# FFT filter and gated FFN in one kernel: the second transform stage as three products of rounded parts, and PSUM banks dealt out three and three

## The chip, the cores and the metric

The kernel runs on one core of one Trainium2 chip. The metric is the time of one execution on the device, in microseconds. Engines are named as in the profile: PE (TensorE, matmuls; PEld are its weight loads), DVE (VectorE), ACT (ScalarE), POOL (GpSimd), and SP (SyncE, which here issues nearly all DMAs).

## The reference

The input `x` has 8 batches of 3136 tokens by 256 channels. Along the tokens a real FFT is taken, multiplied by a complex filter per channel, and transformed back; then comes a gated feed-forward block:

```python
X = np.fft.rfft(x, axis=1)
y = np.fft.irfft(X * (filt_r + 1j * filt_i)[None], n=3136, axis=1)
h = np.maximum(y @ w_in, 0.0)                       # 256 -> 1024
conv_out[:, i] = sum(conv_w[k] * h[:, i + k - 1] for k in range(3))   # along tokens, zeros outside
out = (h / (1 + np.exp(-conv_out))) @ w_out          # 1024 -> 256
```

## The kernel before, in words

**Transforms.** 3136 is 112 x 28, and each batch goes through four stages of matmuls. Stage 1 multiplies by a 112x112 table for each of 28 columns, stage 2 by a small matrix `s2_sb` (112x120, its variant `s2s_sb` for the last column), then the filter is applied, stage 3 multiplies by `s3_sb`/`s3s_sb`, and stage 4 turns the result into `y`, channels on partitions. Each stage is cut into 14 operations of two columns (`NP = 14`). Stage 1 and stage 3 write their results to DRAM (`a_dram`, `b_dram`), since stages 2 and 4 read them in another order. All four stages are plain f32 matmuls; in the trace each f32 matmul stands as two rows.

**Products of parts.** The feed-forward block works on numbers split in two: a high part rounded to f32r by ACT (`hi_act`, L156) and the rest by DVE or POOL (`lo_dve` L159, `lo_pool` L162), both f32r. `mm3` (L186 to L189) multiplies by three matmuls: high by high, high by low, low by high.

**The main loop** (L680) runs over steps m. The tokens of all batches are cut into units of 510 (`UO`); a unit takes 8 steps, one for each 128 of the 1024 inner channels, and a window of 48 steps belongs to one batch. In each step:

- `inner` (L484): 6 matmuls of 512 columns into a bank of the PSUM pool `ps_h`, 4 banks, on PE (L187 to L189, out `ps_h`);
- `relu` and `centre` (ACT, L495 and L500; centre writes the tile `t`, 4 buffers), two taps (DVE, L504), `sigmoid` (ACT, L507), `gate` (DVE, L510, the last reader of the `ps_h` bank, two steps after the inner product), `round_g` (ACT, L156) and `rest_g` (POOL, L162, the last reader of `t`);
- six steps later `project` (L529): 12 matmuls of 256 columns (L536 to L538); after each eighth step `evacuate` copies the output on DVE (L549) and stores it.

Each engine runs its instructions in the order in which the loop issues them (`manual_schedule`), SP's DMAs too.

**The transforms of the next batch** are spread over the steps by a planner (L570 to L600). Window t (t = 1 to 7) holds stages 2 to 4 of batch t and stage 1 of batch t+1, the last window's 48 and more steps hold none. In the second to seventh window stage 2 stands in steps 2, 3, 5, 7, 9, 11, 12, 14, 16, 18, 20, 21, 23 and 25, each stage 3 operation three steps after its stage 2, stage 4 in steps 33 to 44, and stage 1 of the next batch (not in the seventh window) in steps 0, 1, 4, 6, 8, 10, 13, 22, 27, 29, 30, 31, 32 and 45. In the first window two operations of stage 1 of batch 1 stand in each of steps 0 to 5, and stage 2 is denser, two of every three steps from 9 on, often beside a stage 3. Within a step the order is:

```python
for op in old:          # transforms of the step before
    from_bank(op)       # 1, 3: ACT copy (L240) and store; 2: filter on DVE (L264-L266) and POOL (L267); 4: DVE copy (L663)
want_in()               # loads of inputs
for op in new:
    transform(op)       # matmuls into a bank of ps_t
inner(...)
```

`transform` (L631) takes a bank of the PSUM pool `ps_t`, 2 banks, and `from_bank` (L652) empties it one step later. `want_in` (L613) keeps up to five inputs loaded ahead in the tile `tin` (5 buffers); tables and filters are loaded a few operations ahead (`want_table`, `want_filter`). The matmul lines of the transforms are L245 (stage 1), L249 and L252 (stages 2 and 3) and L275 (stage 4), all with out `ps_t`.

**Before the main loop** a prologue transforms batch 0, does two operations of stage 1 of batch 1, and converts the weights. The last quarter of the weights is converted in the first steps of the main loop (`late`).

Of the kernel before, what the change touches and what calls it, by code (L numbers as in the profile page):

```python
# [9 lines left out]
F32 = mybir.dt.float32  # L10
F32R = mybir.dt.float32r
# [121 lines left out]
def tile_fft_filter_gated_ffn(  # L133
# [21 lines left out]
    def hi_act(dst, src):  # L155
        nc.scalar.activation(dst, src, AF.Copy)  # L156
# [33 lines left out]

    dram = ctx.enter_context(tc.tile_pool(name="dram", bufs=1, space=bass.MemoryType.DRAM))
    a_dram = [dram.tile([N2, 112, D], F32, name=f"a_dram{b}") for b in range(B)]
    b_dram = [dram.tile([N2, 112, D], F32, name=f"b_dram{b}") for b in range(B)]
    a_out = [t[:].rearrange("n p d -> p n d") for t in a_dram]
    a_in = [t[:].rearrange("n (r g) d -> (n r) g d", g=G) for t in a_dram]
    b_out = [t[:].rearrange("n (r g) d -> (n r) g d", g=G) for t in b_dram]
    b_in = [t[:].rearrange("n p d -> p n d") for t in b_dram]
    xt = x.rearrange("b (p n) d -> (b p) n d", n=N2)
# [2 lines left out]
    wc = ctx.enter_context(tc.tile_pool(name="wc", bufs=1))  # L201
    s2_sb = wc.tile([112, 120], F32, name="s2_sb")
    s2s_sb = wc.tile([112, 120], F32, name="s2s_sb")
    s3_sb = wc.tile([120, 112], F32, name="s3_sb")
    s3s_sb = wc.tile([120, 112], F32, name="s3s_sb")
    one_sb = wc.tile([128, 128], F32, name="one_sb")
    cw = wc.tile([128, 3, NF], F32, name="cw")
    nc.gpsimd.memset(cw[:, 0, 0:1], 0.0)
    nc.scalar.activation(cw[:, 0, 0:1], cw[:, 0, 0:1], AF.Sigmoid)
# [20 lines left out]
    def pair(q):  # L230
        return slice(2 * q, 2 * q + 2)

    def load_in(pool, kind, b, q, bufs, tag):
        r = pool.tile([112, 2, D], F32, name=tag, bufs=bufs)
        nc.sync.dma_start(out=r, in_={"1": xv, "2": a_in, "4": b_in}[kind][b][:, pair(q)])
        return r

    def store(pool, kind, b, q, ps, bufs, tag, queue=nc.sync):
        st = pool.tile([112, 2, D], F32, name=tag, bufs=bufs)
        nc.scalar.activation(st, ps[0:112].rearrange("p (j d) -> p j d", d=D), AF.Copy)  # L240
        queue.dma_start(out={"1": a_out, "3": b_out}[kind][b][:, pair(q)], in_=st)

    def by_column(ps, w, r):
        for j in range(2):
# [8 lines left out]

    def second(ps, q, r):
        by_row(ps[0:120], q, r, s2_sb, s2s_sb)

    def third(ps, q, z):
        by_row(ps[0:112], q, z, s3_sb, s3s_sb)
# [24 lines left out]
    conv_raw = tp.tile([128, 1, 6 * NF], I32, name="conv_raw", bufs=1)  # L283

    def load_weights(k, pool):
        raws[k] = raw = pool.tile([128, 2, 1024], I32, name="raw", bufs=1 if pool is tp else 2)
        for part, w in enumerate((w_in, w_out)):
            nc.sync.dma_start(out=raw[:, part], in_=w[:, 1024 * k:1024 * k + 1024])

# [3 lines left out]
        e, m = (em[:, i, 0:1, 0:n] for i in range(2))  # L293
        yield from to_f32(cw.rearrange("p (o k) f -> p o (k f)", o=1), conv_raw, e, m)

    def convert(k, pool, n=2):

        for j in range(2):
            em = pool.tile([128, 2, 2, 256], I32, name="em", bufs=n)
            w = pool.tile([128, 2, 256], F32, name="ws", bufs=n)  # L300
            yield from to_f32(w, raws[k][:, :, 512 * j:512 * j + 512], em[:, 0], em[:, 1])
            halves = [(t[0][:, j, 256 * k:256 * k + 256], t[1][:, 2 * k + j]) for t in zip(wi, wo)]
            for part in range(2):
                nc.gpsimd.tensor_copy(halves[0][part], w[:, part])
            for part in range(2):
                lo_pool(halves[1][part], w[:, part], halves[0][part])
# [5 lines left out]
    with (  # L312
# [2 lines left out]
        tc.manual_schedule(engines=COMPUTE | {mybir.EngineType.SP}),  # L315
    ):
        fts, tabs, rows, zs, pss = {}, {}, {}, {}, {}
        by_r = [sc.tile([120, 4, N2], F32, name=f"by_r{i}", bufs=1) for i in range(2)]
        bt = sc.tile([128, KT, G, 112], F32, name="bt", bufs=1)

# [30 lines left out]
        with tc.tile_pool(name="sq", bufs=2) as sq:  # L351
# [14 lines left out]

            def first_loads(c):
                table("1", c)
                r = sq.tile([128, 4, D], F32, name="rows", bufs=5)
                nc.sync.dma_start(out=r, in_=xt[0:128, 4 * c:4 * c + 4])  # L370
                rows["x", c] = r[0:112]
                if c in (0, 3):
                    load_weights(c // 3, sc)
                if c == 1:
                    nc.sync.dma_start(out=conv_raw[:, 0], in_=conv_w)
                if c == 4:
                    for dst, t in ((one_sb, one), (s2_sb, s2[:, 0:120]), (s2s_sb, s2s[:, 0:120]), (s3_sb, s3), (s3s_sb, s3s)):
                        nc.sync.dma_start(out=dst, in_=t)
# [16 lines left out]
            for i in range(NP + 4):  # L395
                if i < NP:
                    back = [at[:, k].rearrange("p n (r g) -> p (n r) g", g=G) for k in range(KT)]
                    rows["2", i] = turn_back(lambda j, k: back[k][:, :, 2 * i + j], sq, "ar")
                if 0 <= i - 1 < NP:
                    pss[i - 1] = ps = bank()  # L400
                    second(ps, i - 1, rows.pop(("2", i - 1)))
                if 0 <= i - NP < AHEAD:
                    ps = bank()
                    by_column(ps, tab("1", i - NP), rows.pop(("1", i - NP)))
                    store(tp, "1", 1, i - NP, ps, 3, "st", nc.scalar)
                if 0 <= i - 4 < NP:
                    q = i - 4
                    ps = turned_stage(zs.pop(q), [by_r[q == NP - 1 and j].rearrange("p r c -> p (r c)") for j in range(2)])
                    nc.scalar.activation(bt[:, :, pair(q)], ps, AF.Copy)
                if 0 <= i - 2 < NP:  # L410
                    zs[i - 2] = filt(pss.pop(i - 2), i - 2, fts.pop(i - 2))
                    if i + 2 < NP:
                        load_filter(i + 2)
                if i == 5:
                    table("1", 0)
                    for q in range(AHEAD):
                        r = sq.tile([128, 2, D], F32, name="xa", bufs=2)
# [24 lines left out]

    yps.append(ctx.enter_context(tc.tile_pool(name="y_odd", bufs=1, reuse_waits="tile")))
    wp = ctx.enter_context(tc.tile_pool(name="wp", bufs=2, reuse_waits="tile"))
    ps_h = ctx.enter_context(tc.tile_pool(name="ps_h", bufs=4, space=bass.MemoryType.PSUM, reuse_waits="tile"))
    ps_t = ctx.enter_context(tc.tile_pool(name="ps_t", bufs=2, space=bass.MemoryType.PSUM, reuse_waits="tile"))
    ps_o = ctx.enter_context(tc.tile_pool(name="ps_o", bufs=1, space=bass.MemoryType.PSUM, reuse_waits="tile"))

    outf = out.rearrange("b s d -> (b s) d")
    LEN = B * ROW - 1  # L450
    NU = -(-LEN // UO)
    ts, hs, gs, pos, joined = {}, {}, {}, {}, {}
    ring = [[wp.tile([128, UO + 66], F32R, name=f"g{i}{h}", bufs=1) for h in range(2)] for i in range(4)]
    for pair_of in ring:
        for g in pair_of:
            nc.gpsimd.memset(g[:, UO:UO + 2].bitcast(F32), 0.0)
# [154 lines left out]
        return kind == "1" or stored.get(({"2": "1", "4": "3"}[kind], b), 0) == NP  # L611

    def want_in():  # L613
        while wanted["in"] < min(done["in"] + 5, len(inputs)) and ready(inputs[wanted["in"]]):
            op = inputs[wanted["in"]]
            wanted["in"] += 1
            got_in[op] = load_in(tp, *op, 5, "tin")

    def want_table(n):
        for op in tables[n:n + 1]:  # L620
# [10 lines left out]
    def transform(op):  # L631
        kind, b, q = op
        banks[op] = ps = ps_t.tile([128, 512], F32, name="ps_t")
        if kind in "124":
            done["in"] += 1
            r = got_in.pop(op)
        if kind in "14":
            want_table(done["table"] + 3)
            done["table"] += 1
            w = got_table.pop(op)  # L640
        if kind == "1":
            by_column(ps, w, r)
        if kind == "2":
            want_filter(done["filter"] + 1)
            done["filter"] += 1
            second(ps, q, r)
        if kind == "3":
            third(ps, q, got_z.pop((b, q)))
        if kind == "4":
            fourth(ps, r, w)  # L650

    def from_bank(op):  # L652

        kind, b, q = op
        ps = banks.pop(op)
        if kind in "13":
            store(tp, kind, b, q, ps, 3, "st")
# [16 lines left out]
    with tc.manual_schedule(engines=COMPUTE | {mybir.EngineType.SP}):  # L674
# [1 line left out]
        for n in range(3):  # L676
            want_table(n)
        want_filter(0)
        late = convert(3, wp, 1)
        for m in range(NF * NU + PLAG + 1):  # L680
            p1, p2, p3, p4, p6, p7 = (at(m - k) for k in (1, 2, 3, 4, PLAG, PLAG + 1))
            new, old = plan.get(m, []), plan.get(m - 1, [])
            if p7:
                evacuate(*p7)
            for op in old:
                from_bank(op)
            want_in()
# [72 lines left out]
```

## Time and profile before

| | |
|---|---|
| median of 3 runs | 1554.89 us (1553.32 to 1556.66) |
| the profiled execution's own time | 1554.59 us |
| its span in the trace | 1552.8 us |
| mean granted TensorE clock | 0.997 |
| first inner product | at 88.85 us |
| bytes moved by DMA | 229.49 MB, mean 148 GB/s |
| HBM read and written | 157.10 MB and 70.65 MB |

The span is what the trace covers; the 1.8 us between it and the execution's own time lie around it. Times in rows are microseconds from the start of the span, a row's second number is its duration, and "x2" means that neighbouring rows were merged. Square brackets give the idle time of the engine before a row and what ended it. Rows of groups give busy time in us and the mean of one in ns, then idle time before them. The ends of matmuls are modelled, so matmul rows overlap; the distance of their starts tells the pace.

### The profile page before, as it was taken

What the parts mean: (1) busy time and instruction counts of PE and PEld (TensorE: products, weight loads), DVE (VectorE), ACT (ScalarE), POOL (GpSimd) and SP (SyncE); (2) the same over time, 40 slices, a digit from 0 to 9 for tenths busy, and PEclk for the clock granted to TensorE, in tenths of its full rate; (3) what the DMA queues carried; (4) which work ended last, traced back from release to release, by engine and by line L of the source; (5) the groups of instructions that cost most, each with busy time, mean ns of one, the idle gap of its engine ahead of it and who ended that gap; (6) DMA issues with size and microseconds to landing.
All of it is one profiled execution on the core that took longest, in us unless ns stands there. A gap on an engine that the chain in (4) does not pass through costs nothing.

```text
span 1552.8 us, 26446 instructions
## 1 busy us (share of the span) xinstructions
PE 1519.7 (98%) x9202; PEld 1290.6 (83%) x9202; DVE 1185.3 (76%) x1810; ACT 1144.7 (74%) x1973; POOL 828.3 (53%) x721
## 2 busy tenths in 40 slices
PE   6999999999999999999999999999999999999999
PEld 5777788877997789877898778987799878999998
DVE  7978766788677877778777776778867888777776
ACT  3576668766896668866787667976688667888886
POOL 4644447545574555645565445744557445664444
PEclk9999999999999999999999999999999999999999
DMA  8867653665436555465544665356543543300000
GB/s 302 256 185 215 208 170 109 181 200 166 135 110 202 179 155 159 121 193 169 177 124 143 185 196 153 97 179 203 165 135 100 160 140 110 101 28 15 28 28 30
DMA packets 158436, 229.49 MB, mean 148 GB/s; under 512 B 16432, under 2 KB 109088, under 8 KB 158304
## 3 DMA queue, kind: packets, MB, share of 16 engines
q1 hardware_dynamic: 157824, 227.35, 48.4%
q8 instruction: 73, 1.20, 0.3%
q14 instruction: 59, 0.48, 0.1%
q10 hardware_dynamic: 480, 0.46, 0.1%
HBM read 157.10 MB, written 70.65 MB: 147 GB/s over the span
## 4 chain that ended last, share of the span: by engine, by line
PE 92%; DVE 2%; ACT 2%; DMA 2%; issue 2%; SPq 0%; POOL 0%; ACTq 0%; POOLq 0%; DVEq 0%
PE ps_h L187 12%; PE ps_h L189 12%; PE ps_h L188 12%; PE po L536 12%; PE po L538 12%; PE po L537 11%; PE ps_t L249 10%; PE ps_t L275 6%; PE ps_t L245 5%; DMA rows<-in_x 1%; PE ps_t L252 1%; ACT br L346 0%; DVE v L265 0%; DVE z L264 0%; DMA f<-in_filt 0%
## 5 line engine op out<-in xcount | busy, mean ns | idle before, releaser
L504 DVE SCALAR_TENSOR_TENSOR t<-ps_h,cw,t 128x510 f32<-128x510 f32 (+1 forms) x800 | 589.1, 737 | 301.5 <-ACT t L500 298.4
L162 POOL TENSOR_TENSOR g<-t,g 128x510 fp32r<-128x510 f32 (+1 forms) x400 | 505.3, 1273 | 203.6 <-ACT g L156 191.9
L536 PE MATMUL po<-wo,g 128*128 128x256 f32 (+1 forms) x1576 | 440.4, 279 | 0.1
L538 PE MATMUL po<-wo,g 128*128 128x256 f32 (+1 forms) x1576 | 439.5, 279 | 0.0
L537 PE MATMUL po<-wo,g 128*128 128x256 f32 (+1 forms) x1576 | 439.3, 279 | 0.0
L495 ACT ACTIVATE ps_h<-ps_h 128x512 f32<-128x512 f32 (+1 forms) x400 | 234.7, 587 | 243.9 <-PE ps_h L189 242.2
L500 ACT ACTIVATE t<-ps_h,cw 128x510 f32<-128x510 f32 (+1 forms) x400 | 272.4, 681 | 102.8 <-POOL g L162 70.1
L267 POOL TENSOR_TENSOR z<-z,v 120x512 f32<-120x512 f32 x112 | 144.8, 1293 | 380.4 <-DVE v L266 312.7
L187 PE MATMUL ps_h<-y,wi 128*128 128x512 f32 (+1 forms) x688 | 333.4, 485 | 0.5 <-DVE y L159 0.5
L536 PEld LDWEIGHTS po<-wo,g 128*128 128x128 f32 (+1 forms) x1576 | 297.0, 188 | 17.3 <-ACT g L156 0.3
L537 PEld LDWEIGHTS po<-wo,g 128*128 128x128 f32 (+1 forms) x1576 | 296.4, 188 | 17.0
L538 PEld LDWEIGHTS po<-wo,g 128*128 128x128 f32 (+1 forms) x1576 | 296.6, 188 | 0.6 <-POOL g L162 0.5
L189 PE MATMUL ps_h<-y,wi 128*128 128x512 f32 (+1 forms) x688 | 270.1, 393 | 0.0
L188 PE MATMUL ps_h<-y,wi 128*128 128x512 f32 (+1 forms) x688 | 270.1, 393 | 0.0
L510 DVE TENSOR_TENSOR t<-ps_h,t 128x510 f32<-128x510 f32 (+1 forms) x400 | 268.6, 671 | 0.9 <-ACT t L507 0.8
L507 ACT ACTIVATE t<-t 128x510 f32<-128x510 f32 (+1 forms) x400 | 245.3, 613 | 1.7 <-DVE t L504 1.6
L156 ACT ACTIVATE g<-t 128x510 fp32r<-128x510 f32 (+1 forms) x400 | 245.1, 613 | 0.2 <-DVE t L510 0.2
L162 POOL TENSOR_TENSOR y<-z,y 128x448 fp32r<-128x448 f32 x98 | 138.5, 1422 | 93.8 <-ACT y L156 91.9
L187 PEld LDWEIGHTS ps_h<-y,wi 128*128 128x128 f32 x688 | 130.4, 189 | 44.3 <-issue 23.6
L188 PEld LDWEIGHTS ps_h<-y,wi 128*128 128x128 f32 x688 | 130.7, 190 | 41.3 <-issue 24.3
L189 PEld LDWEIGHTS ps_h<-y,wi 128*128 128x128 f32 x688 | 130.0, 189 | 30.2 <-POOL wi L162 0.3
L240 ACT ACTIVATE st<-ps_t 112x512 f32<-112x512 f32 x194 | 114.0, 590 | 11.2 <-PE ps_t L245 11.1
(91 smaller groups left out, 1608.0 us busy)
## 6 DMA issues: line engine op xcount, KB each, us to landing
filt<-in_filt SPq DMA_DIRECT2D x98, 512.0 KB
tin<-a_dram SPq DMA_DIRECT2D x98, 224.0 KB
b_dram<-st SPq DMA_DIRECT2D x98, 224.0 KB
tin<-b_dram SPq DMA_DIRECT2D x98, 224.0 KB
tin<-in_x SPq DMA_DIRECT2D x96, 224.0 KB
a_dram<-st SPq DMA_DIRECT2D x96, 224.0 KB
out<-ot SPq DMA_DIRECT2D x45, 256.0 KB
tab<-in_m SPq DMA_DIRECT2D x98, 98.0 KB
```

Source lines behind the costliest of these rows:

```text
L156: nc.scalar.activation(dst, src, AF.Copy)
L162: nc.gpsimd.tensor_tensor(out=dst, in0=src, in1=hi.bitcast(F32), op=ALU.subtract)
L187: nc.tensor.matmul(ps, lhsT=wh, rhs=rh, start=start, stop=False, **kw)
L188: nc.tensor.matmul(ps, lhsT=wh, rhs=rl, start=False, stop=False, **kw)
L189: nc.tensor.matmul(ps, lhsT=wl, rhs=rh, start=False, stop=stop, **kw)
L500: nc.scalar.activation(t, hs[u, f][:, 1:n + 1], AF.Copy, scale=cw[:, 1, f:f + 1])
L504: nc.vector.scalar_tensor_tensor(out=t, in0=h[:, k:place(u)[2] + k], scalar=cw[:, k, f:f + 1], in1=t, op0=ALU.mult, op1=ALU.add)
L507: nc.scalar.activation(ts[u, f], ts[u, f], AF.Sigmoid)
L510: nc.vector.tensor_mul(ts[u, f], hs.pop((u, f))[:, 1:place(u)[2] + 1], ts[u, f])
L536: nc.tensor.matmul(o, lhsT=gh[:, c:c + n], rhs=wo[0][:, f], start=first, stop=False, skip_group_check=True)
L537: nc.tensor.matmul(o, lhsT=gh[:, c:c + n], rhs=wo[1][:, f], start=False, stop=False, skip_group_check=True)
L538: nc.tensor.matmul(o, lhsT=gl[:, c:c + n], rhs=wo[0][:, f], start=False, stop=last, skip_group_check=True)
```

## The change

From the third batch on (b = 2 to 7, six batches of 14 operations) the second stage is done with `mm3`: three f32r matmuls of parts in place of one f32 matmul. The parts of its input are made where the first stage's sums leave PSUM: ACT's copy becomes `hi_act` into the first half of a new tile `sh` (2 buffers), DVE makes the rest with `lo_dve` from the PSUM bank into the second half, and both halves are stored and loaded, by way of a second DRAM tensor `r_dram`. The matrices are split on POOL at step 8. Batches 0 and 1 keep the f32 form.

The PSUM pools change from 4 and 2 banks (`ps_h`, `ps_t`) to 3 and 3.

To make room in SBUF, buffers are dealt out anew: inputs of stage 2 have the tile `tia` (3 buffers), those of stages 1 and 4 `tin` (3 buffers, was 5 for all), stage 3's copies `st` (2 buffers, was 3 for stages 1 and 3); the late weight conversion borrows `tia` and `st`; the prologue's `rows` has 4 buffers (was 5). `want_in` looks six ahead in place of five but holds at most three inputs of either kind, and stops at the first that has no room.

```diff
-    def load_in(pool, kind, b, q, bufs, tag):
-        r = pool.tile([112, 2, D], F32, name=tag, bufs=bufs)
-        nc.sync.dma_start(out=r, in_={"1": xv, "2": a_in, "4": b_in}[kind][b][:, pair(q)])
+    def load_in(pool, kind, b, q):
+        if kind == "2" and b == 1:
+            r = pool.tile([112, 2, 2, D], F32R, name="tia", bufs=3)[:, 0].bitcast(F32)
+            nc.sync.dma_start(out=r, in_=a_in[b][:, pair(q)])
+            return r
+        if kind == "2":
+            r = pool.tile([112, 2, 2, D], F32R, name="tia", bufs=3)
+            for h, t in enumerate((a_in, r_in)):
+                nc.sync.dma_start(out=r[:, h].bitcast(F32), in_=t[b][:, pair(q)])
+            return r
+        r = pool.tile([128, 2, D], F32, name="tin", bufs=3)[0:112]
+        nc.sync.dma_start(out=r, in_={"1": xv, "4": b_in}[kind][b][:, pair(q)])
         return r
...
+    def store_first(pool, b, q, ps, queue=nc.sync):
+
+        st = pool.tile([112, 2, 2, D], F32R, name="sh", bufs=2)
+        p = ps[0:112].rearrange("p (j d) -> p j d", d=D)
+        hi_act(st[:, 0] if b > 1 else st[:, 0].bitcast(F32), p)
+        queue.dma_start(out=a_out[b][:, pair(q)], in_=st[:, 0].bitcast(F32))
+        if b > 1:
+            lo_dve(st[:, 1], p, st[:, 0])
+            queue.dma_start(out=r_out[b][:, pair(q)], in_=st[:, 1].bitcast(F32))
+
+    def store_third(pool, b, q, ps):
+        st = pool.tile([128, 2, D], F32, name="st", bufs=2)[0:112]
         nc.scalar.activation(st, ps[0:112].rearrange("p (j d) -> p j d", d=D), AF.Copy)
-        queue.dma_start(out={"1": a_out, "3": b_out}[kind][b][:, pair(q)], in_=st)
+        nc.sync.dma_start(out=b_out[b][:, pair(q)], in_=st)
...
+    def second_split(ps, q, r):
+
+        if q < NP - 1:
+            mm3(ps[0:120], *second_parts[0], *(r[:, h].rearrange("p j d -> p (j d)") for h in range(2)))
+        else:
+            for j, parts in enumerate(second_parts):
+                mm3(ps[0:120, j * D:j * D + D], *parts, r[:, 0, j], r[:, 1, j])
...
-                r = sq.tile([128, 4, D], F32, name="rows", bufs=5)
+                r = sq.tile([128, 4, D], F32, name="rows", bufs=4)
...
-    ps_h = ctx.enter_context(tc.tile_pool(name="ps_h", bufs=4, space=bass.MemoryType.PSUM, reuse_waits="tile"))
-    ps_t = ctx.enter_context(tc.tile_pool(name="ps_t", bufs=2, space=bass.MemoryType.PSUM, reuse_waits="tile"))
+    ps_h = ctx.enter_context(tc.tile_pool(name="ps_h", bufs=3, space=bass.MemoryType.PSUM, reuse_waits="tile"))
+    ps_t = ctx.enter_context(tc.tile_pool(name="ps_t", bufs=3, space=bass.MemoryType.PSUM, reuse_waits="tile"))
...
-        while wanted["in"] < min(done["in"] + 5, len(inputs)) and ready(inputs[wanted["in"]]):
+        while wanted["in"] < min(done["in"] + 6, len(inputs)) and ready(inputs[wanted["in"]]):
             op = inputs[wanted["in"]]
+            if sum((o[0] == "2") == (op[0] == "2") for o in got_in) == 3:
+                break
             wanted["in"] += 1
-            got_in[op] = load_in(tp, *op, 5, "tin")
+            got_in[op] = load_in(tp, *op)
...
-            second(ps, q, r)
+            (second_split if b > 1 else second)(ps, q, r)
...
+            if m == NF:
+                for (h, l), t in zip(second_parts, (s2_sb, s2s_sb)):
+                    nc.gpsimd.tensor_copy(h, t)
+                    lo_pool(l, t, h)
```

More of the change, by code (lines that the diff above doesn't have):

```diff
@@ L192, in tile_fft_filter_gated_ffn @@
     a_dram = [dram.tile([N2, 112, D], F32, name=f"a_dram{b}") for b in range(B)]
+    r_dram = [dram.tile([N2, 112, D], F32, name=f"r_dram{b}") for b in range(B)]
     b_dram = [dram.tile([N2, 112, D], F32, name=f"b_dram{b}") for b in range(B)]
-    a_out = [t[:].rearrange("n p d -> p n d") for t in a_dram]
-    a_in = [t[:].rearrange("n (r g) d -> (n r) g d", g=G) for t in a_dram]
+    a_out, r_out = ([t[:].rearrange("n p d -> p n d") for t in ts] for ts in (a_dram, r_dram))
+    a_in, r_in = ([t[:].rearrange("n (r g) d -> (n r) g d", g=G) for t in ts] for ts in (a_dram, r_dram))
     b_out = [t[:].rearrange("n (r g) d -> (n r) g d", g=G) for t in b_dram]
@@ L203, in tile_fft_filter_gated_ffn @@
     s2s_sb = wc.tile([112, 120], F32, name="s2s_sb")
+    second_parts = [[wc.tile([112, 120], F32R, name=f"{n}{h}") for h in range(2)] for n in ("s2", "s2s")]
     s3_sb = wc.tile([120, 112], F32, name="s3_sb")
     s3s_sb = wc.tile([120, 112], F32, name="s3s_sb")
-    one_sb = wc.tile([128, 128], F32, name="one_sb")
     cw = wc.tile([128, 3, NF], F32, name="cw")
@@ L231, in pair @@
         return slice(2 * q, 2 * q + 2)
-    def load_in(pool, kind, b, q, bufs, tag):
-        r = pool.tile([112, 2, D], F32, name=tag, bufs=bufs)
-        nc.sync.dma_start(out=r, in_={"1": xv, "2": a_in, "4": b_in}[kind][b][:, pair(q)])
-        return r
-    def store(pool, kind, b, q, ps, bufs, tag, queue=nc.sync):
-        st = pool.tile([112, 2, D], F32, name=tag, bufs=bufs)
+    def load_in(pool, kind, b, q):
[10 more added lines that the diff above has]
+        nc.sync.dma_start(out=r, in_={"1": xv, "4": b_in}[kind][b][:, pair(q)])
+        return r
+    def store_first(pool, b, q, ps, queue=nc.sync):
[8 more added lines that the diff above has]
+        st = pool.tile([128, 2, D], F32, name="st", bufs=2)[0:112]
         nc.scalar.activation(st, ps[0:112].rearrange("p (j d) -> p j d", d=D), AF.Copy)
-        queue.dma_start(out={"1": a_out, "3": b_out}[kind][b][:, pair(q)], in_=st)
+        nc.sync.dma_start(out=b_out[b][:, pair(q)], in_=st)
     def by_column(ps, w, r):
@@ L285, in load_weights @@
     def load_weights(k, pool):
-        raws[k] = raw = pool.tile([128, 2, 1024], I32, name="raw", bufs=1 if pool is tp else 2)
+        if pool is tp:
+            raws[k] = [pool.tile([128, 2, 2, D], F32R, name="tia", bufs=3).rearrange("p a j d -> p a (j d)").bitcast(I32) for _ in range(2)]
+            for j in range(2):
+                for part, w in enumerate((w_in, w_out)):
+                    nc.sync.dma_start(out=raws[k][j][:, part], in_=w[:, 1024 * k + 512 * j:1024 * k + 512 * j + 512])
+            return
+        raws[k] = raw = pool.tile([128, 2, 1024], I32, name="raw", bufs=2)
         for part, w in enumerate((w_in, w_out)):
@@ L294, in convert_conv, with convert @@
         yield from to_f32(cw.rearrange("p (o k) f -> p o (k f)", o=1), conv_raw, e, m)
-    def convert(k, pool, n=2):
+    def convert(k, pool):
         for j in range(2):
-            em = pool.tile([128, 2, 2, 256], I32, name="em", bufs=n)
-            w = pool.tile([128, 2, 256], F32, name="ws", bufs=n)
-            yield from to_f32(w, raws[k][:, :, 512 * j:512 * j + 512], em[:, 0], em[:, 1])
+            if pool is tp:
+                if j == 0:
+                    em = pool.tile([128, 2, 2, D], F32R, name="tia", bufs=3).bitcast(I32)
+                w, raw = pool.tile([128, 2, D], F32, name="st", bufs=2), raws[k][j]
+            else:
+                em = pool.tile([128, 2, 2, 256], I32, name="em", bufs=2)
+                w, raw = pool.tile([128, 2, 256], F32, name="ws", bufs=2), raws[k][:, :, 512 * j:512 * j + 512]
+            yield from to_f32(w, raw, em[:, 0], em[:, 1])
             halves = [(t[0][:, j, 256 * k:256 * k + 256], t[1][:, 2 * k + j]) for t in zip(wi, wo)]
@@ L317, in tile_fft_filter_gated_ffn @@
         fts, tabs, rows, zs, pss = {}, {}, {}, {}, {}
+        one_sb = sc.tile([128, 128], F32, name="one_sb", bufs=1)
         by_r = [sc.tile([120, 4, N2], F32, name=f"by_r{i}", bufs=1) for i in range(2)]
@@ L404, in tile_fft_filter_gated_ffn @@
                     by_column(ps, tab("1", i - NP), rows.pop(("1", i - NP)))
-                    store(tp, "1", 1, i - NP, ps, 3, "st", nc.scalar)
+                    store_first(tp, 1, i - NP, ps, nc.scalar)
                 if 0 <= i - 4 < NP:
@@ L416, in tile_fft_filter_gated_ffn @@
                     for q in range(AHEAD):
-                        r = sq.tile([128, 2, D], F32, name="xa", bufs=2)
+                        r = tp.tile([128, 2, D], F32, name="tin", bufs=3)
                         nc.sync.dma_start(out=r, in_=xt[N1:N1 + 128, pair(q)])
@@ L452, in tile_fft_filter_gated_ffn @@
     ts, hs, gs, pos, joined = {}, {}, {}, {}, {}
-    ring = [[wp.tile([128, UO + 66], F32R, name=f"g{i}{h}", bufs=1) for h in range(2)] for i in range(4)]
+    ring = [[wp.tile([128, UO + 2], F32R, name=f"g{i}{h}", bufs=1) for h in range(2)] for i in range(4)]
     for pair_of in ring:
@@ L655, in from_bank @@
         ps = banks.pop(op)
+        if kind == "1":
+            store_first(tp, b, q, ps)
+        if kind == "3":
+            store_third(tp, b, q, ps)
         if kind in "13":
-            store(tp, kind, b, q, ps, 3, "st")
             stored[kind, b] = stored.get((kind, b), 0) + 1
@@ L678, in tile_fft_filter_gated_ffn @@
         want_filter(0)
-        late = convert(3, wp, 1)
+        late = convert(3, tp)
         for m in range(NF * NU + PLAG + 1):
```

## The prediction

> **What bounds the kernel now.** I read the page first: engine shares and the chain that ended last.
>
> ```profile
> PE 1519.7 (98%) x9202; PEld 1290.6 (83%) x9202; DVE 1185.3 (76%) x1810; ACT 1144.7 (74%) x1973; POOL 828.3 (53%) x721
> ...
> PE 92%; DVE 2%; ACT 2%; DMA 2%; issue 2%; SPq 0%; POOL 0%; ACTq 0%; POOLq 0%; DVEq 0%
> ```
>
> TensorE (PE) is busy for 98% of the span and makes 92% of the chain. VectorE (DVE) and ScalarE (ACT) come next with a quarter of the span free. So a microsecond of PE work is worth about one of the kernel's time, unless PE was waiting there. As ends of matmuls are modelled, waits are read better from the distance of one step's last inner-product matmul (the second L189 of a step) to that of the next. The PE timeline in the last batch, where there is no transform, gives the bare step:
>
> ```profile
> 1402.48 0.39 PE L189 MATMUL ps_h<-yx,wi 128*128 128x512 f32 x1
> ...
> 1405.24 0.39 PE L189 MATMUL ps_h<-yx,wi 128*128 128x512 f32 x1
> ```
>
> 2.76 us for 6 products of 512 columns and 12 of 256, 6144 columns in all, so 0.23 us for 512 columns of a product of parts. Next, the same view early in the second 48-step window (transforms of the third batch):
>
> ```profile
> 296.50 0.39 PE L189 MATMUL ps_h<-yx,wi 128*128 128x512 f32 x1
> ...
> 301.00 0.39 PE L189 MATMUL ps_h<-yx,wi 128*128 128x512 f32 x1
> ...
> 304.36 1.12 PE L245 MATMUL ps_t<-tin,tab 112*112 112x256 f32 x4 [0.72 <-ACT st L240]
> ...
> 306.47 0.39 PE L189 MATMUL ps_h<-yx,wi 128*128 128x512 f32 x1
> ...
> 310.11 0.39 PE L189 MATMUL ps_h<-yx,wi 128*128 128x512 f32 x1
> ...
> 315.11 0.40 PE L189 MATMUL ps_h<-y,wi 128*128 128x512 f32 x1
> ```
>
> By the plan, the four intervals hold a third and a second stage (4.50 us), a third and a first (5.47), a second alone (3.64), a third and a first (5.00). From 4.50 and 2.76 a plain f32 operation of 512 columns costs 0.87 us; 3.64 says 0.88. Two operations should give 4.50 each time. The 5.47 and 5.00 are 0.97 and 0.50 us of PE waiting. The row at 304.36 shows where: the second operation of a step wants the bank that the step before used, and it is not yet emptied. That is the two-bank `ps_t`.
>
> **Part by part.** *The products.* The second stage's 0.87 us become three products of parts at 0.23: 0.70, so 0.17 less. Its last pair, in halves of 256, has the same columns. Six batches of 14 are 84 operations: −14.3 us. Between 0 and that if PE waits there.
>
> *Three banks for transforms.* The two waits above, 1.47 us together, stand in windows two to six: −7.3 us in five windows. With a third bank the second operation of a step takes a bank emptied a step earlier, or follows 0.7 to 0.9 us later. In the first window the same pattern shows thrice (a third and a second stage, 4.50 us expected), and once in the fourth stage:
>
> ```profile
> 133.42 0.39 PE L189 MATMUL ps_h<-y,wi 128*128 128x512 f32 x1
> ...
> 139.20 0.39 PE L189 MATMUL ps_h<-y,wi 128*128 128x512 f32 x1
> ...
> 147.32 0.39 PE L189 MATMUL ps_h<-y,wi 128*128 128x512 f32 x1
> ...
> 153.31 0.39 PE L189 MATMUL ps_h<-y,wi 128*128 128x512 f32 x1
> ...
> 174.23 0.39 PE L189 MATMUL ps_h<-y,wi 128*128 128x512 f32 x1
> ...
> 179.71 0.39 PE L189 MATMUL ps_h<-y,wi 128*128 128x512 f32 x1
> ...
> 243.21 1.12 PE L275 MATMUL ps_t<-tab,tin 112*128 112x112 f32 x8 [1.36 <-issue]
> ```
>
> 5.78, 5.99 and 5.48 are 1.28, 1.49 and 0.98 over; with 1.36 that is 5.1 us. In the seventh window one such wait is long:
>
> ```profile
> 1242.06 0.39 PE L189 MATMUL ps_h<-y,wi 128*128 128x512 f32 x1
> ...
> 1246.90 2.03 PE L249 MATMUL ps_t<-tin,s_sb 112*120 112x512 f32 x2 [2.17 <-issue]
> ...
> 1250.61 0.40 PE L189 MATMUL ps_h<-y,wi 128*128 128x512 f32 x1
> ```
> ```profile
> 1246.90:1250.30 3.40, 3.40 (x6) 2.06 (x7) 3.25 (x5) 0.00 (x0) 2.47 (x2) 0.50 0.68 161
> ```
>
> 8.55 us for 4.50 expected: 2.17 idle, then (the stretch row) 3.40 us at a granted clock of 0.50, which costs half, 1.7. Together −4.0 us. Sum for this edit: −16.4 us; from 0, if the waits only move, to that.
>
> *Three banks for the inner product.* The inner product of step m now waits for the gate (L510) of step m−3, not m−4. How near is that? A DVE row and a PE row of the second stage of a later batch, gate of m−3 and inner product of m:
>
> ```profile
> 556.03 0.68 DVE L510 TENSOR_TENSOR t<-ps_h,t 128x510 f32<-128x510 f32 x1
> ```
> ```profile
> 557.44 0.80 PE L187 MATMUL ps_h<-y,wi 128*128 128x512 f32 x1
> ```
>
> The gate ends at 556.71, 0.73 us before. This is among the tightest places of these windows, at an output evacuation (L549) and two filters in a row on DVE. PE now comes earlier there by 0.17 for each second stage just before it, so I expect waits of tenths: 0.5 us a window in six windows and 1 us in the first, +4 us; from 0 to 12 (2 us a window). Behind a waiting inner product stand all later PE instructions, so such a wait is paid in full.
>
> *Parts at the first stage's sums.* ACT's copy becomes the rounding at the same size. New is a DVE difference for 84 operations, from PSUM, 112x512.
>
> ```profile
> L510 DVE TENSOR_TENSOR t<-ps_h,t 128x510 f32<-128x510 f32 x392 | 266.5, 680 | 0.5 <-ACT t L507 0.5
> ```
> ```profile
> L159 DVE TENSOR_TENSOR y<-ps,y 128x448 fp32r<-128x448 f32 x14 | 13.8, 1030 | 1.1 <-ACT y L156 1.0
> ```
> ```profile
> DVE t L504 <- ACT t L500: 298.4, 265, 3.7
> ```
>
> It costs between 0.68 us (the gate, contiguous output) and 1.03 us (the same subtraction with a strided output); I take 0.68, as its output is contiguous: 57 us of DVE, to 87. Its cover: before its first tap DVE waits 298.4 us for ACT's centre copy, 265 times, 1.1 us each, and the difference stands just ahead of that tap while ACT still does relu and centre. In this plan no first stage falls in a step with a second one, so no filter is in the same DVE step. Taken at zero; uncovered it is 57 us. One stretch row, steps 2 to 28 of the third window, says that there is room:
>
> ```profile
> 468.90:573.00 104.10, 103.13 (x557) 81.50 (x556) 83.31 (x126) 68.85 (x123) 49.58 (x40) 1.00 0.62 185
> ```
>
> DVE 83.3 of 104.1 us, plus seven differences 88. The second store and load of each operation, 224 KB each, are two more SP instructions behind that difference; DMA share is 0.62, and three buffers hold second-stage inputs some five steps ahead. Taken at zero, up to +3.
>
> *Fewer input buffers at the start.* First-stage inputs had five buffers; now they have three, two operations a step run in steps 0 to 5 without projections, and the load that refills a buffer stands on SP behind the stores of the same step. SP and PE rows:
>
> ```profile
> 89.39 0.95 SPq L235 DMA_DIRECT2D tin<-in_x  x2
> ...
> 94.52 0.92 SPq L623 DMA_DIRECT2D tab<-in_s  x2
> ```
> ```profile
> 90.33 1.89 PE L245 MATMUL ps_t<-tin,tab 112*112 112x256 f32 x8
> ...
> 98.58 1.09 PE L245 MATMUL ps_t<-tin,tab 112*112 112x256 f32 x4 [0.96 <-DMA tab<-in_s]
> ...
> 106.18 1.09 PE L245 MATMUL ps_t<-tin,tab 112*112 112x256 f32 x4 [0.60 <-ACT t L500]
> ```
>
> The table issued at 94.52 ended a wait at 98.58: up to 4 us from issue to use. For an input I take 3 (DMA will be less crowded). The load at 89.39 now serves the second operation of step 1, due at 91.2 (half of the row at 90.33): 92.4 instead. After that each step is operation (0.9) → ACT copy and two store issues (about 1.7, by the distance of end 91.2+0.9 to the next loads after 93) → landing 3: 5.5 us. Today the second operation goes from 91.2 to 106.18 in four steps, 3.75 each. So 1.2 + 4 × 1.75 = +8 us; from +4 (landing 2) to +13 (landing 4). The waits of some 2 us may also drop the clock, as the one at 1246.90 did; PE is not the bound in those steps, so I add 1: +9. [...]
>
> *The rest.* The rounding of the stage's matrices at step 8 puts four small operations on GpSimd (POOL), which also serves the ring: +1. The prologue's fourth row buffer waits for the same matmuls as its table, which had four buffers already: nothing.
>
> Sum: −14.3 − 16.4 + 4 + 9 + 1 = −16.7. The profiled execution took 1554.59 us (span 1552.8), 0.3 below the median of the runs, 1554.89. That gives 1538 us.
>
> **Rivals.** *The loop outside PE becomes the bound (1558 us).* While second stages run every other step, filter (DVE), sum and ring difference (POOL), centre (ACT), tap and gate (DVE) form a circle over two steps. In the seventh window, where no first stage of a next batch gives it time, ACT's centre copies waited for POOL at this distance:
>
> ```profile
> 1227.33 0.69 ACT L500 ACTIVATE t<-ps_h,cw 128x510 f32<-128x510 f32 x1 [2.50 <-POOL g L162]
> ...
> 1234.70 0.69 ACT L500 ACTIVATE t<-ps_h,cw 128x510 f32<-128x510 f32 x1 [2.37 <-POOL g L162]
> ```
>
> 7.37 us for two steps, where PE needs 2 × 3.64 today and 7.11 after. With one bank fewer for the inner product PE cannot run ahead of it. If this holds in all windows, the bank waits come back as waits for the gate and half of the products' gain goes too: −7 + 9 + 1, about +3. Against it: in windows two to six 14 first stages of 0.9 us give the circle slack, and the gates ended 0.7 us and more early.
>
> *The difference is not covered (1591 us).* If DVE is late when it comes, each of the 84 pushes a gate by 0.68 us and, with three banks, PE: −16.7 + 57 − 4 = +36. It decides where DVE's wait before the tap is shorter than 0.68 us; the mean of 1.1 speaks against.
>
> *Everything is covered (1524 us).* Loads land within 2 us, gates stay ahead: −30.7.
>
> *The products bring nothing (1552 us).* If three products of 112 rows ran no faster than one in f32; the 0.23 us of L188 and L189 speak against.
>
> **How the numbers follow.** Forecast 0.66, loop 0.14, uncovered difference 0.04, all covered 0.13, no gain from products 0.03. Forecast alone spans 1528 to 1549 by the bounds of start and gate waits. The range, 1524 to 1552, leaves out most of the loop's and the difference's cases. A measurement of this kernel can tell about 0.2%, 3.1 us. Faster: 0.66 + 0.13 + 0.03 and a little of the loop's, 0.83; same: 0.05, from the loop's; slower: 0.12.
>
> **What would show it.** Products: second-stage steps without other transforms at 3.46 instead of 3.64 us. Banks: intervals like 5.47 and 5.00 near 4.50, and no 2 us wait in the seventh window. Gates: inner products whose wait is ended by DVE L510. Start: first-stage matmuls in steps 1 to 5 waiting for `tin`, and the sixth step's inner product later by 9 us. Difference: 0.68 us, and DVE's wait before the tap shorter by it. I am wrong if the start stays as it is, or if PE's waits for L510 come to more than 12 us.

## The result and the profile after

The changed kernel took 1548.06 us (median of 5 runs, 1545.57 to 1548.69), the kernel before 1555.2 us beside it (median of 5, 1553.32 to 1557.21). The ratio is 0.995 with a 95% interval of 0.9935 to 0.9964: faster by 7 us, where 17 had been forecast. The profiled execution took 1547.31 us, its span 1545.5.

First the page of the kernel after: busy time of the engines, and the chain that ended last.

```profile
PE 1509.5 (98%) x9292; PEld 1308.4 (85%) x9292; DVE 1233.9 (80%) x1894; ACT 1144.9 (74%) x1973; POOL 830.5 (54%) x725
...
PE 87%; DVE 4%; issue 3%; DMA 3%; ACT 2%; POOL 1%; SPq 0%; POOLq 0%; ACTq 0%; DVEq 0%
```

PE is 10 us less busy than before and the span is 7 us shorter. The chain says more than that: PE's share fell from 92% to 87%, and DVE, DMA, POOL and issue took it. PE waits for other things than before.

The prediction named rows that would show it. The first is the distance of step ends in the PE timeline of the second window (third and second stage, third and first, second alone, third and first):

```profile
305.98 0.39 PE L189 MATMUL ps_h<-yx,wi 128*128 128x512 f32 x1
...
310.31 0.40 PE L189 MATMUL ps_h<-yx,wi 128*128 128x512 f32 x1
...
314.82 0.39 PE L189 MATMUL ps_h<-yx,wi 128*128 128x512 f32 x1
...
318.29 0.40 PE L189 MATMUL ps_h<-yx,wi 128*128 128x512 f32 x1
...
322.82 0.40 PE L189 MATMUL ps_h<-y,wi 128*128 128x512 f32 x1
```

4.33, 4.51, 3.47 and 4.53 us, before 4.50, 5.47, 3.64 and 5.00. The second stage gives 0.17 as forecast, and both bank waits are gone.

The second is the start. The PE rows are the second first-stage operation of steps 0 to 5, the SP rows what stood ahead of one of them in the queue:

```profile
90.22 1.12 PE L265 MATMUL ps_t<-tin,tab 112*112 112x256 f32 x4 [1.22 <-DVE y L159]
...
95.93 1.09 PE L265 MATMUL ps_t<-tin,tab 112*112 112x256 f32 x4 [2.33 <-DMA tin<-in_x]
...
101.42 1.75 PE L265 MATMUL ps_t<-tin,tab 112*112 112x256 f32 x4 [2.14 <-ACT sh L156]
...
107.59 1.09 PE L265 MATMUL ps_t<-tin,tab 112*112 112x256 f32 x4 [1.22 <-DMA tin<-in_x]
...
113.43 1.09 PE L265 MATMUL ps_t<-tin,tab 112*112 112x256 f32 x4 [2.48 <-DMA tin<-in_x]
...
118.99 2.02 PE L265 MATMUL ps_t<-tin,tab 112*112 112x256 f32 x4 [2.19 <-ACT sh L156]
```
```profile
97.06 0.60 ACT L156 ACTIVATE sh<-ps_t 112x512 f32<-112x512 f32 x1 [2.38 <-PE ps_t L265]
...
97.68 0.32 SPq L253 DMA_DIRECT2D a_dram<-sh  x1
...
98.06 0.93 SPq L245 DMA_DIRECT2D tin<-in_x  x2
```

The circle can be read off: the operation ends at 97.02, ACT copies it (97.06 to 97.66), SP stores (97.68), loads (98.06), and 3.4 us after that the next operation starts (101.42). Its wait is put down to ACT's next copy, but that one had ended 0.65 us earlier; the distance from the load is that of its neighbour (92.37 to 95.93, 3.6 us). Five such distances make 28.77 us, 5.75 each; 5.5 was forecast.

The third is the fourth stage, which the prediction did not ask for and for which it had no term. PE's waits for inputs over the whole kernel (engine, line and releaser, then us in total, times and the longest), the PE timeline around step 39 of the second window, and SP's queue there:

```profile
PE ps_t L265 <- DMA tin<-in_x: 6.0, 3, 2.5
...
PE ps_t L303 <- DMA tin<-b_dram: 3.1, 5, 1.3
```
```profile
436.61 0.39 PE L189 MATMUL ps_h<-y,wi 128*128 128x512 f32 x1
...
438.22 1.04 PE L303 MATMUL ps_t<-tab,tin 112*128 112x112 f32 x8
439.56 1.12 PE L303 MATMUL ps_t<-tab,tin 112*128 112x112 f32 x8 [0.30 <-issue]
...
441.69 0.39 PE L189 MATMUL ps_h<-y,wi 128*128 128x512 f32 x1
```
```profile
434.79 0.40 SPq L594 DMA_DIRECT2D out<-ot  x1
435.60 0.83 SPq L607 DMA_DIRECT2D out<-ot  x2
436.55 0.33 SPq L245 DMA_DIRECT2D tin<-b_dram  x1
```

This step holds two operations of the fourth stage and takes 5.08 us; before it took 4.55. The load of an input was issued right behind three stores of the output, 1.7 us ahead of the first and 3.0 ahead of the second operation.

The fourth is the third and the seventh window, steps 3 to 29. Before, then after; the columns are the stretch, its length, busy time of PE, PEld, DVE, ACT and POOL, the granted clock, the DMA share and GB/s:

```profile
473.90:581.03 107.13, 106.16 (x577) 84.56 (x576) 85.82 (x130) 72.94 (x130) 53.50 (x44) 1.00 0.59 177
...
1209.29:1312.32 103.03, 100.45 (x545) 79.44 (x544) 84.31 (x128) 67.39 (x121) 52.10 (x43) 0.98 0.42 128
```
```profile
480.37:583.71 103.34, 103.34 (x592) 86.61 (x590) 89.69 (x137) 72.53 (x130) 53.42 (x44) 1.00 0.76 225
...
1203.43:1303.35 99.92, 98.56 (x559) 80.44 (x558) 84.44 (x129) 66.80 (x122) 52.25 (x43) 1.00 0.54 163
```

In the third window these steps fell from 107.13 to 103.34 us, with PE busy throughout. In the seventh window the gain is only 3.1, and 1.4 us of idle PE stay.

The gates, as the prediction asked: weight loads of the inner product that waited for the gate (L550 here) over the whole kernel, in us, times and the longest.

```profile
PEld ps_h L187 <- DVE t L550: 7.0, 18, 1.0
```

That is below the 12 us named as a sign of being wrong, and 6.2 of it stand in the seventh window. The difference takes 0.68 us, and DVE's wait before its first tap fell from 298.4 to 252.7 us.

Where the 7.3 us went, by the end of the last inner product of each step in both traces:

| stretch | forecast | measured |
|---|---|---|
| until the first step's end | 0 | +2.2 |
| first window, steps 1 to 6 | +9 | +12.0 |
| rest of the first window (waits for banks −5.1, gate +1, split +1) | −3.1 | −4.4 |
| windows 2 to 6, steps 1 to 29 (products −11.9, banks −7.3, gate +2.5) | −16.7 | −21.0 |
| windows 2 to 6, steps 30 on: fourth stage (+5.0) and end (+0.6) | 0 | +5.5 |
| window 7 (products −2.4, bank −4.0, gate +0.5) | −5.9 | −2.3 |
| last window | 0 | +0.7 |
| sum | −16.7 | −7.3 |

### The profile page after: what moved, and what is told of

Read it like the earlier page. It is cut to its first block, busy times and chain, and to the rows that moved or that the text cites. A ratio compares the mean times of both kernels' runs of the same rounds, so it can differ in the third digit from the quotient of the medians.

```text
span 1545.5 us, 26909 instructions
## 1 busy us (share of the span) xinstructions
PE 1509.5 (98%) x9292; PEld 1308.4 (85%) x9292; DVE 1233.9 (80%) x1894; ACT 1144.9 (74%) x1973; POOL 830.5 (54%) x725
## 3 DMA queue, kind: packets, MB, share of 16 engines
q8 instruction: 74, 1.21, 0.4%
## 4 chain that ended last, share of the span: by engine, by line
PE 87%; DVE 4%; issue 3%; DMA 3%; ACT 2%; POOL 1%; SPq 0%; POOLq 0%; ACTq 0%; DVEq 0%
PE ps_h L187 11%; PE ps_h L189 11%; PE ps_h L188 11%; PE po L576 11%; PE po L578 11%; PE po L577 11%; PE ps_t L269 5%; PE ps_t L303 5%; PE ps_t L265 5%; PE ps_t L187 1%; PE ps_t L188 1%; PE ps_t L189 1%; DMA tin<-b_dram 1%; POOL g L162 1%; DMA tin<-in_x 1%
## 5 line engine op out<-in xcount | busy, mean ns | idle before, releaser
L544 DVE SCALAR_TENSOR_TENSOR t<-ps_h,cw,t 128x510 f32<-128x510 f32 (+1 forms) x800 | 588.6, 736 | 256.3 <-ACT t L540 252.7
L187 PE MATMUL ps_h<-y,wi 128*128 128x512 f32 (+1 forms) x688 | 312.5, 454 | 1.8 <-DVE t L550 1.7
L188 PE MATMUL ps_h<-y,wi 128*128 128x512 f32 (+1 forms) x688 | 270.3, 393 | 0.0
L189 PE MATMUL ps_h<-y,wi 128*128 128x512 f32 (+1 forms) x688 | 270.1, 393 | 0.0
L550 DVE TENSOR_TENSOR t<-ps_h,t 128x510 f32<-128x510 f32 (+1 forms) x400 | 268.6, 672 | 1.1 <-ACT t L547 0.8
L265 PE MATMUL ps_t<-tin,tab 112*112 112x256 f32 x384 | 100.6, 384 | 11.6 <-DMA tin<-in_x 6.0
```

Of the source, the lines that this page charges most:

```text
L187: nc.tensor.matmul(ps, lhsT=wh, rhs=rh, start=start, stop=False, **kw)
L188: nc.tensor.matmul(ps, lhsT=wh, rhs=rl, start=False, stop=False, **kw)
L189: nc.tensor.matmul(ps, lhsT=wl, rhs=rh, start=False, stop=stop, **kw)
L544: nc.vector.scalar_tensor_tensor(out=t, in0=h[:, k:place(u)[2] + k], scalar=cw[:, k, f:f + 1], in1=t, op0=ALU.mult, op1=ALU.add)
L550: nc.vector.tensor_mul(ts[u, f], hs.pop((u, f))[:, 1:place(u)[2] + 1], ts[u, f])
```

## Experiments

The theory after the result: the two gains are real, and what is missing went to input buffers (start and fourth stage, because the refill stands on SP behind stores) and to the seventh window, where the loop outside PE is the bound. The rival: the difference on DVE and its second stores and loads, not the buffers, eat the gain. The split below means the products of parts with all that belongs to them: rounding, difference, second stores and loads. The first four kernels below ran beside a kernel before of 1555.22 us, the last three beside one of 1554.45.

**Loads ahead of stores.** The changed kernel with one more refill of the input buffers at the head of each step:

```diff
             new, old = plan.get(m, []), plan.get(m - 1, [])
+            want_in()
             if p7:
                 evacuate(*p7)
```

> The changed kernel with one more call of the input loads at the head of each step, ahead of the output and transform stores on SP; nothing else differs. Theory A (the loss at the start and the waits in the fourth stage come from loads that stand behind stores on SP, with three buffers): steps 0 to 5 take about 24 us instead of 32.5, steps with two fourth-stage operations go back from 4.9 to 4.6 us, in all 10 to 13 us faster than the change, about 1536 us. Rival B (three buffers are too few whatever the order, or the two buffers of the first stage's sums hold ACT): steps 0 to 5 stay above 30 us and the time within 3 us of the change's 1548.

1531.66 us (1530.7 to 1532.09), ratio 0.9849 [0.9832, 0.9865] against the kernel before: 16.4 us less than the change alone, from one line, and more than the 10 to 13 expected. SP's loads in the start:

```profile
93.37 0.95 SPq L245 DMA_DIRECT2D tin<-in_x  x2
94.75 1.47 SPq L253 DMA_DIRECT2D a_dram<-sh  x2
...
97.30 1.87 SPq L245 DMA_DIRECT2D tin<-in_x  x2
...
101.51 0.98 SPq L245 DMA_DIRECT2D tin<-in_x  x2
```

The loads follow each other in 3.9 and 4.2 us, and PE's wait for `in_x` over the whole kernel is 3.0 us in place of 6.0. Steps 1 to 6 took 21.66 us instead of 32.52 (before: 20.50), the waits for `b_dram` are gone, and the fourth stages and window ends of windows two to six got 4.6 of their 5.5 us back. With the start on time, steps 7 to 12 take 1.6 us longer, where weight loads of the inner product wait 2.9 us for the gate.

**Only the buffers.** The changed kernel with four and two banks again, and the second stage, its difference and its second stores and loads undone, so that new tiles, buffers and the order of loads stay:

```diff
-        hi_act(st[:, 0] if b > 1 else st[:, 0].bitcast(F32), p)
+        hi_act(st[:, 0].bitcast(F32), p)
...
-        if b > 1:
-            lo_dve(st[:, 1], p, st[:, 0])
-            queue.dma_start(out=r_out[b][:, pair(q)], in_=st[:, 1].bitcast(F32))
...
-            (second_split if b > 1 else second)(ps, q, r)
+            second(ps, q, r)
...
-    ps_h = ... bufs=3 ...
-    ps_t = ... bufs=3 ...
+    ps_h = ... bufs=4 ...
+    ps_t = ... bufs=2 ...
```

(and `kind == "2"` in place of `kind == "2" and b == 1` at the load).

> The new buffers alone: inputs of three and three, two buffers for the first stage's sums, four prologue row buffers, the conversion in borrowed tiles, the loads' new rule; but second stage in f32 for all batches, no differences, no second stores, and banks four and two as before. Theory A: slower than the kernel before by what the start and the fourth stage lost, 12 + 5 us, so about 1570 us. Rival C (the loss belongs to the split, to its second loads and stores): within 5 us of the kernel before.

1567.18 us (1566.26 to 1568.98), ratio 1.008 [1.0065, 1.0095]: the buffers alone cost 12 us. The start makes most of it (steps 1 to 6 in 31.03 us, +10.5, and the first step ends 4.1 later). So for the start the rival falls: there the loss is there without any split. The fourth stages of windows two to six lose only 1.8 us here, where the change lost 5.0; the run with the old banks, below, has split and buffers together and shows 4.7. There both theories share: the buffers open the wait, and the split lengthens it. Most of what it adds, 2.4 us in the changed kernel against nothing here, stands in step 33, right behind the last first stages. In the fifth window's step 33 PE waits 1.25 us for `tin` from `b_dram`: on SP, stores to `a_dram` (at 953.54, 2.16 us long) and `r_dram` (955.79) stand ahead of that load (956.29), which comes 3.4 us behind the end of step 31; with the buffers alone it comes 0.1 us behind it. What lengthens step 39, where most of the rest stands, is open.

**Only the banks.** The kernel before with three banks each:

```diff
-    ps_h = ... bufs=4 ...
-    ps_t = ... bufs=2 ...
+    ps_h = ... bufs=3 ...
+    ps_t = ... bufs=3 ...
```

> The kernel before with nothing but three and three banks. If the gate waits stay small: bank waits gone, 5 us in the first window, about 8 in windows two to six, 4 in the seventh, so 15 to 17 us faster than the kernel before, about 1539 us, less than the whole change took. Rival D: within 4 us of the kernel before, with waits for the gate in place of those for banks.

1540.14 us (1539.68 to 1540.59), ratio 0.9905 [0.989, 0.9919]: 15 us faster, by itself twice the whole change. Third window, seventh window, and the weight loads that waited for the gate:

```profile
468.53:574.21 105.68, 105.68 (x577) 84.73 (x576) 85.85 (x130) 72.83 (x130) 53.53 (x44) 1.00 0.59 177
1196.65:1296.70 100.05, 99.14 (x546) 78.44 (x544) 84.28 (x128) 66.98 (x122) 52.11 (x43) 1.00 0.44 132
```
```profile
PEld ps_h L187 <- DVE t L510: 8.6, 17, 1.7
```

The third window's steps 3 to 29 fell from 107.13 to 105.68 us and PE no longer waits there. The seventh window has with banks alone all but 0.13 us of what the change has (99.92).

**The change with the old banks.**

```diff
-    ps_h = ... bufs=3 ...
-    ps_t = ... bufs=3 ...
+    ps_h = ... bufs=4 ...
+    ps_t = ... bufs=2 ...
```

> The changed kernel with the banks as before, four for the inner product and two for transforms. If the third transform bank is worth what the step intervals say: the waits of 0.97 and 0.50 us in steps 6 and 8 and those of the first and seventh window come back, 14 to 20 us slower than the change, about 1564 us. Rival D (three inner-product banks cost as much as the third transform bank gives): within 4 us of the change's 1548.

1573.52 us (1572.81 to 1574.75), ratio 1.012 [1.0105, 1.0135]: not only 25.5 us over the change, where 14 to 20 were expected, but 6.3 over the buffers alone. With two transform banks the products gain nothing: steps 1 to 29 of windows two to six take 2.2 us more than with the buffers alone. The rest of the 6.3 has other places: 2.9 in the fourth stages and ends of these windows and 1.8 in the seventh, where no first stage stands, less 0.9 at the start. The third window, the weight loads that waited for a difference, and step 14 of the second window in the timeline:

```profile
486.83:594.66 107.83, 104.73 (x591) 85.95 (x590) 90.18 (x137) 73.14 (x130) 53.65 (x44) 1.00 0.74 217
```
```profile
PEld ps_t L187 <- DVE sh L159: 11.4, 10, 1.8
```
```profile
346.63 0.40 PE L189 MATMUL ps_h<-y,wi 128*128 128x512 f32 x1
...
347.77 1.40 DVE L589 COPY ot<-po 128x512 f32<-128x512 f32 x2 [0.78 <-PE po L578]
...
349.09 0.68 DVE L159 TENSOR_TENSOR sh<-ps_t,sh 112x512 fp32r<-112x512 f32 x1
...
349.84 0.18 PEld L187 LDWEIGHTS ps_t<-tia,s 112*120 112x120 f32 x1 [1.38 <-PE ps_t L269]
...
351.81 0.40 PE L189 MATMUL ps_h<-y,wi 128*128 128x512 f32 x1
```

5.18 us for a step that takes 4.40 after and 4.55 before (4.51 with the buffers alone). A bank now has two readers, ACT's rounding and DVE's difference, and the second stands on DVE behind the output copy of 1.40 us. The weight load at 349.84 is put down to PE, but what ended just before it, at 349.77, is the difference. In steps 14 and 23 of each of windows two to six PE is idle for 0.57 and 0.90 to 0.94 us until within 0.1 us of a difference's end, 7.4 us together; with the buffers alone it is not idle there. In the third window PE is idle for 3.1 of 107.83 us, where it was never idle with three banks. So three and three banks are worth 15 us without the split (and with five input buffers) and 25.5 with it (and three); the steps 1 to 29 of windows two to six give 8.9 of the one and 22.0 of the other.

**The products alone.** Loads ahead of stores as above, three banks each, and the second stage in f32 again, with the edits of the buffers' experiment other than the banks.

> Early loads and three and three banks, with the products undone: second stage in f32 for all batches, no differences, no second stores. If the products are worth 0.17 us an operation wherever no bank is waited for: about 12 us slower than the same kernel with products (1532), so about 1544 us. If with three transform banks the products bring nothing either: 1532 us.

1542.89 us (1542.19 to 1543.37), ratio 0.993 [0.9913, 0.9946]. Against 1531.66 the split is worth 11.2 us by the medians, which stand beside two different kernels before, 0.8 apart; by the ends of the last step in the two traces, 10.4. The third and the seventh window of this kernel:

```profile
470.82:576.02 105.20, 105.20 (x578) 84.27 (x577) 85.64 (x130) 72.76 (x130) 53.46 (x44) 1.00 0.59 176
1198.46:1298.58 100.12, 99.11 (x546) 78.16 (x544) 84.33 (x129) 66.92 (x122) 52.16 (x43) 1.00 0.46 137
```

In the third window 1.8 us are the products' (105.20 against 103.40 with loads ahead), in the five windows two to six 1.7 to 2.5, near the 13 × 0.17 = 2.2 of these steps. In the seventh window it is 0.2 (100.12 against 99.90), though the same 13 operations stand in it.

**The difference twice.** Loads ahead of stores, and DVE makes the difference of each first stage two times (the second writes the same values):

```diff
             lo_dve(st[:, 1], p, st[:, 0])
+            lo_dve(st[:, 1], p, st[:, 0])
```

> The changed kernel with early loads, and the difference of the first stage's sums done twice on DVE, 57 us more of DVE work; only time is asked of it. If DVE's wait before its first tap covers the difference with room to spare: less than 4 us slower than the same kernel with one difference (1532). If the difference is on the path: about 50 us slower. In between, 10 to 20 us: covered once, but not twice.

1538.54 us (1537.35 to 1539.95), ratio 0.9901 [0.9886, 0.9916]: 6.9 us over 1531.66 (5.5 by the last step of the traces) for 58 us more of DVE work. That is none of the three expected outcomes: more than the 4 us of a difference covered with room to spare, less than the 10 to 20 of one that is covered once only. The rows of its operations and of DVE's wait before the tap show where it went. First with loads ahead alone, then with the difference twice:

```profile
L159 DVE TENSOR_TENSOR sh<-ps_t,sh 112x512 fp32r<-112x512 f32 x84 | 57.4, 683 | 4.3 <-ACT sh L156 4.2
```
```profile
DVE t L544 <- ACT t L540: 239.3, 248, 4.0
```
```profile
L159 DVE TENSOR_TENSOR sh<-ps_t,sh 112x512 fp32r<-112x512 f32 x168 | 115.4, 687 | 4.7 <-ACT sh L156 1.8
```
```profile
DVE t L545 <- ACT t L541: 190.4, 197, 4.1
```

Of the added 58.0 us the wait before the tap gave 48.9. What shows in the time stands mainly at the window ends: the last two steps of a window and the first of the next take 0.7 us more in the first window and in each of windows two to six (4.4 in all), where the first stage of step 45 leaves its difference.

**Early loads in the kernel before**, the line of the first experiment in the old kernel:

> The kernel before, with only the input loads issued ahead of the stores. Theory A says that with five buffers a load has a step more to land, so the order hardly matters: within 3 us of the kernel before. If the order itself is worth something: 5 us or more faster.

1555.01 us (1552.37 to 1556.53), ratio 1.0001 [0.9992, 1.0011]. With five input buffers the order of loads and stores is worth nothing; the 16.4 us belong to the three buffers.

More input buffers in the changed kernel, or a third `sh`, were not tried.

## Why the prediction was right and wrong

16.7 us were forecast and 7.3 came, by the traces. That 1548 us still lies in the stated range is in part luck, for large errors cancel. The buffers cost 8.0 us more than priced (3.0 in the start, 5.0 in the fourth stage), the first step 2.2, the seventh window 3.6 and the window ends and the last window 1.3; the rest of the first window and windows two to six gave 5.6 more than forecast.

**Products, −14.3: right mechanism, 11.2 measured.** 3.64 to 3.47 at the step is the forecast's 0.17 an operation. The shortfall is mostly the seventh window: 14 × 0.17 = 2.4 forecast, some 0.4 found (0.2 in steps 3 to 29, 0.2 before them).

**Three transform banks, −16.4, and three for the inner product, +4: −12.4 forecast, −15 measured** where they stand alone. The trace of that kernel gives −8.9 in steps 3 to 29 of windows two to six (forecast −7.3), −5.1 in the first window after step 12 (forecast −5.1) and −3.0 in the seventh (forecast −4.0). The gate costs show as +1.4 at steps 7 to 12, and about 0.5 each at the ends of the last two windows; in windows two to six there are none. The prediction priced 0.5 us a window there from an end 0.73 us early, and that was too dear.

Of the 4.0 us forecast for the seventh window, 1.7 were the clock drop behind the wait at 1246.90, and another trace does not have that drop. In the kernel before with early loads the same step has the same wait:

```profile
1246.69 1.09 PE L249 MATMUL ps_t<-tin,s_sb 112*120 112x512 f32 x2 [2.18 <-issue]
```

The granted clock stays at 1.00 there, the row takes 1.09 us in place of 2.03, and the step takes 6.95 us in place of 8.55. Against that trace the changed kernel's seventh window is only 0.6 us shorter, not 2.3.

**The difference, taken at zero: right as far as shown.** Doubling it costs 6.9 of 58 us, and that it hides so well suggests that the first one is hidden too; no run took it away by itself. But treating it as an instruction on DVE alone missed its other effect. It is a second reader of the transform's bank, and with two banks PE is idle behind it for the 7.4 us above. In steps 1 to 29 of windows two to six the split saves 10.8 us with three banks (loads ahead of stores) and loses 2.2 with two. Without the third bank the products do not gain, which separate sums for products and banks do not show. How much of this is the second reader, and how much a faster PE that waits longer for a bank that empties no sooner, no run told apart.

**Fewer input buffers, +9: the term that was mis-sized, and it decides the miss.** The mechanism was forecast step by step, with 5.5 us a step where 5.75 came. The sum compared four steps with 3.75 us each; the circle holds for five, and the kernel before runs the first two of them in 3.13 and 3.14 us. And two clock drops came where 1 us was allowed in all. Here is the granted clock around the waits (third column from the end):

```profile
98.30:101.70 3.40, 1.26 (x6) 0.76 (x5) 1.90 (x3) 2.28 (x4) 0.00 (x0) 1.00 0.91 255
101.70:105.10 3.40, 3.40 (x9) 2.60 (x8) 1.66 (x4) 0.60 (x1) 2.56 (x4) 0.50 0.37 103
115.40:118.80 3.40, 1.40 (x7) 0.79 (x5) 1.44 (x3) 2.74 (x5) 3.33 (x6) 1.00 0.76 229
118.80:122.20 3.40, 3.21 (x8) 2.51 (x9) 0.56 (x1) 0.65 (x2) 1.72 (x2) 0.50 0.38 105
```

Around the ends of the waits of 2.14 and 2.19 us the clock falls to 0.50 for 3.4 us, and these two steps took 7.08 and 7.07 us where their neighbours took 5.69 and 5.84; the step behind the first took only 4.57, so about 1.2 us of that drop came back (against 5.75 a step). PE was busy for 1.26 and 1.40 us of the 3.40 before these drops. So the start cost 12.0, and 10.9 of it goes when the loads stand ahead of the stores.

The larger part of this term's error is that only the start was priced. The same three buffers serve the fourth stage, and there the refill comes late behind the output stores: +5.0 us over five windows, in part lengthened by the split, whose second stores and loads the prediction took at zero. The prediction looked at the second stage's new buffers and at the start, and never asked who else uses `tin`. With loads ahead of stores 4.6 of it goes.

**The rival "the loop outside PE becomes the bound": right in the one window where its rows came from.** In the seventh window, where 2.3 us came of 5.9 forecast, this is who waits; kernel before, then after, over the middle of the window:

```profile
ACT t L500 <- POOL g L162: 16.7, 10, 3.3
```
```profile
ACT t L540 <- POOL g L162: 29.2, 14, 3.0
...
PEld ps_h L187 <- DVE t L550: 6.2, 16, 1.0
```

ACT's centre waits 12.5 us more for POOL, and 16 weight loads of the inner product wait for the gate. Most of what the products save PE there turns into waiting. In windows two to six the loop has slack, as the prediction argued: they gave 4.3 us more than forecast. The forecast should have split this rival by windows rather than weigh it for the whole kernel.

**Open:** the first step of the main loop ends 2.2 us later than before (1.6 with loads ahead). One trace is a rough measure of it: that end stands at 89.9 to 91.3 us in the three traces with the old prologue and at 91.7 to 94.2 in the six with the new one. PE's last rows of the prologue are 1.5 us late already (the last row of the fourth stage starts at 86.99, before at 85.48), and PE then waits 1.22 us for `y` of DVE's L159, at 90.22 above, before 0.50. Which of the prologue's edits makes it late was not told apart.

Of the versions that ran, the change with loads ahead of stores is the best: 1531.66 us, 23.6 below the kernel before.

## What to carry to other kernels

When a buffer is taken away, list every stage that uses the tile and price each; then look at what stands ahead of the refill in its queue, since here loads ahead of stores were worth 16.4 us with three buffers and nothing with five. An added reader of a PSUM bank is priced twice, as work on its engine and as a longer hold of the bank (here 57.4 us of DVE, and with two banks 7.4 us of idle PE), so a change of banks and a change of readers are not summed as if they were independent. A gain measured in one window is not multiplied over windows whose bound is another engine's loop (the seventh gave 2.3 of 5.9 us), and a clock drop seen once is not counted as a sure cost (1.7 us here, absent at the same step of another trace).

## What was not expected of the hardware

Two waits, of 2.14 and 2.19 us, came with half the granted clock for 3.4 us; PE was busy for 1.27 and 1.21 of the 3.40 us up to their ends. Longer waits in the same start brought no drop, such as the one of 2.48 us that ends at 113.43. The 3.40 us before that end and behind it:

```profile
110.03:113.43 3.40, 0.92 (x5) 0.45 (x4) 2.89 (x6) 2.79 (x5) 0.00 (x0) 1.00 0.87 247
113.43:116.83 3.40, 3.37 (x14) 2.43 (x14) 1.05 (x3) 1.37 (x3) 2.17 (x4) 1.00 0.53 151
```

PE was busy for only 0.92 us up to that end, and the clock stayed at 1.00. So in this trace neither the length of a wait nor PE's share up to its end tells whether the clock drops.

With the split, whose difference is one more DVE reader of a bank, three and three banks were worth 25.5 us in place of 15, though DVE was far from full (90.18 of 107.83 us in the stretch shown). The two kernels differ in their input buffers too.
